# Loading the first batch's V by runs of four tokens, with half-height mask matmuls and grouped column sums

## The chip, the core and the metric

The kernel runs on one core of a Trainium2 chip. The metric is the device time of one execution in microseconds (us). TensorE is called PE in the profile (PEld is its weight load), VectorE DVE, ScalarE ACT, GpSimd POOL. SyncE, SP, issues the loads and stores; SPq is its queue of them.

## The reference

Sliding-window attention over 8 batches of 8 heads, 576 tokens and 64 channels, then a two-layer network over the 4608 tokens.

```python
scores = scale * np.matmul(q, k.transpose(0, 1, 3, 2))
mask = np.abs(pos[:, None] - pos[None, :]) <= 32
scores = np.where(mask, scores, -1000000000.0)
attn = np.exp(scores - np.max(scores, axis=-1, keepdims=True))
attn = attn / (np.sum(attn, axis=-1, keepdims=True) + 1e-09)
attn_out = np.matmul(attn, v)
x = np.ascontiguousarray(attn_out.transpose(0, 2, 1, 3)).reshape(B * S, H * D)   # 4608 x 512
h = x @ w_in                      # 512 x 2048
r = np.maximum(h, 0.0)
g = s * (r * r) + b               # s and b are single numbers
out = g @ w_out                   # 2048 x 512
```

Since `b` is one number, `b` times the sum of `w_out` over its 2048 rows is a constant row of the output. The kernel computes it apart (`constant`) and adds it at the end.

## The kernel before

**A planner writes the order.** The kernel calls `add(engine, function, cost, reads, writes, key, ...)` for each piece of work. `_Graph.plan` then simulates the five engines and the DMA queue with these costs and picks, for each engine, whichever ready piece starts first (by `key` where several could). `emit` writes each engine's instructions in this order, with semaphore waits only where a buffer's reader or writer on another engine asks for one. The order is fixed at build time. On the chip each engine works it off in sequence and stands still where the next piece isn't ready.

**Names.** In the code the batches are numbered from 0; the texts here say batch one for `b = 0` and batch two for `b = 1`. A unit is 128 tokens of a batch; each batch has four whole ones and a half. `s1` is the first layer: 512 of the 2048 hidden channels (a weight chunk `w0` to `w3`, each loaded in halves `a` and `b`) for a block of tokens, four matmuls to each 128 channels. `second` is the second layer, with seven products in place of eight (`TW` and `GSUM` hold the sums for it).

**The start.** q and k of batch one come by head pairs (`load_pair`, 256 KB each, four tokens to a partition, so in runs of 1 KB), are cast to bf16, transposed on PE (`turn_pair`) and multiplied (`pair_scores`). A mask goes into the score banks first: `SHUT`, which is 0 inside the window and -1e38 outside, is multiplied by the identity `IDENT`, and the score matmuls (64 x 64 tiles) add to it, so that the exponential on ACT gives zeros outside. `stir` adds matmuls of a matrix of ones, whose results are not used.

The other loads of batch one and the first half of `w_in` follow by a written list:

```python
ORDER0 = ("v0", "w0a", "v1", "t", "w0b", "v2", "v3", "w1a", "v4", "w1b")
```

"v0" to "v4" are the units of V (`load_v`: 128 tokens to the partitions, 8 heads to a partition, so runs of 256 B; then one cast each, `cast_v`, by the engine in `EV0`). "t" is the tail of q and k, tokens 512 to 575, in two halves of 64 partitions; `late_scores` needs it, and units 3 and 4 need that. After the list, `first_units` does the five units: the product with V into a PSUM bank, the division (`finish`), a transpose on PE, and the copy to `XT`, from which `s1` reads. `ORDER1` goes on with q, k and V of batch two, the other two chunks of `w_in`, and `w_out`. SP issues all of it from one queue, and a load waits until the casts have left its staging slot (`STG`, a ring).

**The column sums.** `constant` multiplies each 128 x 512 tile of `w_out` by the matrix of ones (16 matmuls of 512 columns into one bank), and DVE multiplies the result by `b`.

**PSUM.** Four pairs of banks: `W` (transposes at the start, then the first layer), `O`, `SC` and `AVN`.

The functions around the change, with the line numbers of the profile:

Of the kernel before, what the change touches and what calls it, by code (L numbers as in the profile page):

```python
# [5 lines left out]
F32 = mybir.dt.float32  # L6
I32 = mybir.dt.int32
BF16 = mybir.dt.bfloat16
# [19 lines left out]
ORDER0 = ("v0", "w0a", "v1", "t", "w0b", "v2", "v3", "w1a", "v4", "w1b")  # L28
# [20 lines left out]
EV0 = ("dve", "act", "pool", "dve", "pool")  # L49
# [6 lines left out]
        ("turn", 3, "q"): 1, ("turn", 3, "k"): 1, ("scores", 2): 1, ("scores", 3): 1, ("av", 0): 1}  # L56
# [266 lines left out]
def bass_sliding_window_symmetric__then__act_starrelu_kernel(  # L323
# [23 lines left out]
    with ExitStack() as es:  # L347
# [49 lines left out]
        IDENT = sb((128, 128), BF16, "ident")  # L397
        GT = [sb((128, 16, 512), BF16, "gt") for _ in range(2)]
# [4 lines left out]
        CVEC = sb((128, DM), F32, "cvec")  # L403
        SB128 = sb((128, 2), F32, "sb128")
# [93 lines left out]
        for p0 in (0, 64):  # L498
            band(MASK[p0:p0 + 64, :], ONESW[p0:p0 + 64, :], ("MASK", 0, p0), 0, 64, -96)

# [34 lines left out]
        def take(what, n):  # L535
            ring[what] += 1
            return (ring[what] - 1) % n
# [63 lines left out]

        def load_pair(name, pr, load_key):
# [7 lines left out]
        def stir(spot, res, view, key):  # L610

            n = STIR.get(spot, 0)
            if n:
                add("pe", [lambda e: e.matmul(view, lhsT=ONESW[:, :], rhs=ONESW[:, :].rearrange("p (one c) -> p one c", one=1)
                                              .to_broadcast((128, 4, 128)), start=True, stop=True) for _ in range(n)],
                    n * (427.0 if spot == ("turn", 0, "q") else 240.0), reads=["ONESW"], writes=[res], key=key - 0.05)
# [288 lines left out]
        def pair_scores(b, pr):  # L905
# [3 lines left out]
            if b == 0:  # L909
# [10 lines left out]
            add("pe", [lambda e, hp=hp: e.matmul(bank[:, hp, :], lhsT=IDENT[:, :], rhs=SHUT.rearrange("p u c -> p (u c)"),  # L920
                                                 start=True, stop=False, skip_group_check=True) for hp in (0, 1)],
                440.0, reads=["IDENT"] + [("SHUT", i) for i in range(4)], writes=[(name, 0), (name, 1)], key=key - 0.01)
# [72 lines left out]
        def attention():  # L995
# [228 lines left out]
        def constant():  # L1224

            for i in range(8):
                f0 = 2 * i
                add("pe", [lambda e, fc=fc: e.matmul(SC[:, 0, :], lhsT=ONESW[:, :], rhs=WOUT_BF[:, fc, :],  # L1228
                                                     start=(fc == 0), stop=(fc == 15)) for fc in (f0, f0 + 1)],
                    440, reads=["ONESW", ("Wout", i // 2, i % 2)], writes=[("SC", 0)], accum=i > 0, key=P2[0, 0] - 4.0 + 0.1 * i)  # L1230
            add("dve", lambda e: e.tensor_scalar(CVEC[:, :], SC[:, 0, :], SB128[:, 1:2], None, ALU.mult),
                680, reads=[("SC", 0), ("SB128", 1)], writes=[("CVEC", x) for x in (0, 1)], key=P2[0, 0] - 2.0)

# [273 lines left out]
```

## Time and profile before

| | |
|---|---|
| time, median of 3 runs | 308.14 us (307.1 to 309.0) |
| the profiled execution's own time | 308.89 us |
| its span in the profile | 307.2 us |
| PE busy | 294.9 us, 96% of the span |
| PEld busy | 213.4 us, 69% |
| DVE busy | 233.2 us, 76% |
| ACT busy | 156.7 us, 51% |
| POOL busy | 66.4 us, 22% |
| moved by the DMA engines | 54.30 MB, mean 177 GB/s |

How such a profile is read: the page gives busy times and groups of instructions. The chain of waits goes back from the last instruction, at each step to whatever released it. A row of a timeline has start, duration, engine, line of code, operation, output and inputs, count, and in brackets the idle time before it with what ended that; for PE, durations overlap, so the distance between starts says what a matmul costs. A row of a window has its length and then the busy time and number of instructions of PE, PEld, DVE, ACT and POOL, the TensorE clock granted (1.00 is full), the mean busy share of the 16 DMA engines, and GB/s.

### The profile page before, as it was taken

What the parts mean: (1) busy time and instruction counts of PE and PEld (TensorE: products, weight loads), DVE (VectorE), ACT (ScalarE), POOL (GpSimd) and SP (SyncE); (2) the same over time, 40 slices, a digit from 0 to 9 for tenths busy, and PEclk for the clock granted to TensorE, in tenths of its full rate; (3) what the DMA queues carried; (4) which work ended last, traced back from release to release, by engine and by line L of the source; (5) the groups of instructions that cost most, each with busy time, mean ns of one, the idle gap of its engine ahead of it and who ended that gap; (6) DMA issues with size and microseconds to landing.
All of it is one profiled execution on the core that took longest, in us unless ns stands there. A gap on an engine that the chain in (4) does not pass through costs nothing.

```text
span 307.2 us, 8786 instructions
## 1 busy us (share of the span) xinstructions
PE 294.9 (96%) x3837; PEld 213.4 (69%) x3837; DVE 233.2 (76%) x401; ACT 156.7 (51%) x244; POOL 66.4 (22%) x79
## 2 busy tenths in 40 slices
PE   8879899999999999999999999989999999999994
PEld 3458687798888887666766666656666666666783
DVE  3556788699879697989798768995877776566673
ACT  3746775685895564655554544542554433333200
POOL 5344587300000270055047000450000000000000
PEclk9979999999999999999999999999999999999999
DMA  7999999999994997999699679999513110210223
GB/s 204 290 246 302 325 291 370 268 227 273 159 232 125 239 202 160 279 201 178 184 255 198 132 172 273 186 201 150 153 21 88 53 47 31 74 34 2 69 70 107
DMA packets 120152, 54.30 MB, mean 177 GB/s; under 512 B 94816, under 2 KB 115936, under 8 KB 120112
## 3 DMA queue, kind: packets, MB, share of 16 engines
q1 hardware_dynamic: 120112, 53.72, 75.0%
q8 instruction: 31, 0.51, 0.8%
q14 instruction: 9, 0.07, 0.1%
HBM read 36.70 MB, written 9.44 MB: 150 GB/s over the span
## 4 chain that ended last, share of the span: by engine, by line
PE 79%; SPq 4%; DMA 3%; DVE 2%; issue 1%; POOL 0%
PE w L1097 36%; PE o L1154 31%; PE avn L839 4%; SPq L714 3%; DMA stg<-in_moe_w_in_dram 2%; PE sc L1154 2%; PE sc L781 2%; PE avn L870 1%; PE sc L1228 1%; DMA vst<-in_v_dram 1%; DVE outs L1170 1%; DVE gt L1110 1%; SPq L887 0%; SPq L707 0%; POOL win L564 0%
## 5 line engine op out<-in xcount | busy, mean ns | idle before, releaser
L1097 PE MATMUL w<-xt,win 128*128 128x512 bf16 (+4 forms) x832 | 145.7, 316 | 1.3 <-POOL win L564 1.3
L1104 ACT ACTIVATE r<-w 128x512 bf16<-128x512 f32 (+2 forms) x148 | 86.6, 586 | 105.6 <-PE w L1097 103.9
L1097 PEld LDWEIGHTS w<-xt,win 128*128 128x128 bf16 x832 | 75.6, 99 | 35.9 <-POOL win L564 1.9
L1110 DVE TENSOR_TENSOR gt<-r 128x1024 bf16<-128x1024 bf16 (+3 forms) x100 | 63.6, 639 | 24.9 <-ACT r L1104 24.2
L1154 PE MATMUL o<-wout,gt 128*128 128x256 bf16 x528 | 66.5, 273 | 0.0
L1154 PEld LDWEIGHTS o<-wout,gt 128*128 128x128 bf16 x528 | 50.8, 98 | 13.3
L733 POOL CAST nat<-stg 128x1024 bf16<-128x1024 f32 (+2 forms) x28 | 33.7, 1202 | 78.8 <-DMA stg<-in_q_dram 65.0
L809 ACT ACTIVATE ex<-sc 128x1024 bf16<-128x1024 f32 (+1 forms) x29 | 29.7, 1023 | 12.4 <-PE avn L839 10.8
L1154 PE MATMUL o<-tw,gt 128*128 128x256 bf16 x272 | 34.6, 273 | 0.0
L1154 PEld LDWEIGHTS o<-tw,gt 128*128 128x128 bf16 x272 | 26.2, 98 | 7.0
L1170 DVE SCALAR_TENSOR_TENSOR outs<-o,sb,cvec 128x512 f32<-128x512 f32 (+1 forms) x36 | 25.7, 715 | 4.3 <-PE o L1154 4.3
L1170 DVE SCALAR_TENSOR_TENSOR outs<-o,sb,outs 128x512 f32<-128x512 f32 (+1 forms) x27 | 19.3, 716 | 6.7 <-PE o L1154 6.6
L1146 DVE TENSOR_TENSOR gt<-gt 128x1024 bf16<-128x1024 bf16 (+1 forms) x26 | 23.8, 916 | 0.4
L813 DVE TENSOR_TENSOR ex<-ex,mask 128x1024 bf16<-128x1024 bf16 (+1 forms) x29 | 22.5, 775 | 0.6
L863 DVE TENSOR_TENSOR xn<-avn,rec 128x512 bf16<-128x512 f32 (+1 forms) x31 | 21.3, 687 | 0.7
L839 PE MATMUL avn<-vb,ex 64*64 64x65 bf16 x944 | 19.9, 197 | 1.9 <-issue 1.6
L839 PEld LDWEIGHTS avn<-vb,ex 64*64 64x64 bf16 x944 | 13.0, 106 | 11.5 <-issue 8.0
L598 DVE CAST vb<-vst 128x512 bf16<-128x512 f32 (+1 forms) x30 | 13.1, 444 | 9.5 <-DMA vst<-in_v_dram 9.5
L1154 PE MATMUL o<-tw,gsum 128*128 128x256 bf16 x136 | 17.7, 273 | 0.0
L1154 PEld LDWEIGHTS o<-tw,gsum 128*128 128x128 bf16 x136 | 12.8, 98 | 3.3
L1146 DVE TENSOR_TENSOR gsum<-gt 128x1024 bf16<-128x1024 bf16 x18 | 13.2, 731 | 0.3
L878 ACT COPY xt<-avn 128x512 bf16<-128x512 bf16 (+2 forms) x19 | 10.0, 533 | 4.8 <-PE avn L870 4.8
(119 smaller groups left out, 225.4 us busy)
## 6 DMA issues: line engine op xcount, KB each, us to landing
vst<-in_v_dram SPq DMA_DIRECT2D x32, 256.0 KB, 4.8
out_dram<-outs SPq DMA_DIRECT2D x32, 256.0 KB, 3.6
stg<-in_k_dram SPq DMA_DIRECT2D x24, 256.0 KB, 6.5
stg<-in_q_dram SPq DMA_DIRECT2D x5, 1024.0 KB, 6.0
stg<-in_moe_w_in_dram SPq DMA_DIRECT2D x8, 512.0 KB, 7.4
stg<-in_moe_w_out_dram SPq DMA_DIRECT2D x8, 512.0 KB, 7.4
stg<-in_q_dram SPq DMA_DIRECT2D x4, 512.0 KB, 8.2
stg<-in_k_dram SPq DMA_DIRECT2D x4, 512.0 KB, 8.4
```

Source lines behind the costliest of these rows:

```text
L598: (lambda e: e.tensor_copy(VB[0:n, vb, :, 0:D], VST[0:n, vs, :, :])),
L733: (lambda e, dst=dst, src=src: e.tensor_copy(dst, src)),
L809: add("act", lambda e, dst=flat_dst, src=flat_src: e.activation(dst, src, AF.Exp, bias=0.0, scale=0.125), 190 + 0.833 * 512 * len(hs), rea ...
L813: add("dve", lambda e, flat=flat, mask=mask: e.tensor_tensor(flat, flat, mask, ALU.mult), 130 + 0.53 * 512 * len(hs), reads=[("E", ei, hp, ...
L839: return [lambda e: e.matmul(av[64 * x:64 * x + 64, h, 0:D + 1], lhsT=buf[64 * g:64 * g + 64, h % 2, h // 2, c:c + 64], rhs=VB[64 * g:64 * ...
L863: add("dve", lambda e: e.tensor_tensor(XN[xi][0:p1, :].rearrange("p (a c) -> p a c", a=H), av[0:p1, :, 0:D], REC[ri][0:p1, :].rearrange("p ...
L1097: add("pe", [lambda e, g=g, kc=kc: e.matmul(wt[:, g, :], lhsT=WIN_BF[:, kc, (f0 + g) * 128:(f0 + g + 1) * 128], rhs=XT[:, kc, t0 % XR:t0 % ...
L1104: add("act", lambda e: e.activation(rt, wt, AF.Relu, bias=0.0, scale=1.0), 190 + 0.833 * ng * nt, reads=[("W", wb)], writes=[("R1", rb, ha ...
L1110: add("dve", lambda e: e.tensor_tensor(GT[gs][:, f1:f1 + nf, g0:g0 + nt], rr, rr, ALU.mult), 130 + 0.55 * nf * nt, reads=[("R1", rb, x) fo ...
L1146: add("dve", lambda e: e.tensor_tensor(dst, x, y, op), 1240.0 if half is None else 690.0, reads=reads, writes=writes, key=k)
L1154: add("pe", [lambda e, g=g, j=j, dst=dst: e.matmul(dst, lhsT=lhs[:, g, 128 * j:128 * j + 128], rhs=rhs[:, g, :], start=first and g == 0 an ...
L1170: add("dve", lambda e, src=src, dst=dst, other=other: e.scalar_tensor_tensor(dst, src, SB128[:, 0:1], other, ALU.mult, ALU.add), 200 + 1.0 ...
```

## The change

It has three parts.

**V of batch one.** The units 0 to 3 come in two loads ("va", "vb", 256 tokens each) instead of four. In each, four tokens in a row go to one partition, for four heads in partitions 0 to 63 and for the other four in 64 to 127, as two DMAs in runs of 1 KB. A cast on DVE brings all 128 x 1024 values to bf16. Sixteen matmuls of 32 rows with a constant pattern of zeros and ones (`SPREAD`) put each token on its own partition, in four banks; two evictions to a load bring them to `VB`. Unit 4 is loaded as before. The list of loads changes, and so does the filling ahead of unit 0 (`STIR`, one matmul to six), which now also waits for the first spread.

**The masks.** `SHUT` has the same rows for partitions 0 to 63 and 64 to 127. The two mask matmuls of a pair of banks now take 64 rows each, the first from the upper half, the second from the lower half, with `TWICE`, two 64 x 64 identities side by side.

**The column sums.** Four matmuls of 32 output columns go to four groups of 32 partitions of one bank, four rounds in all. ACT copies the four partial sums out, a float32 matmul with a matrix of 1/32 adds them up, and DVE multiplies by `b`.

```diff
-ORDER0 = ("v0", "w0a", "v1", "t", "w0b", "v2", "v3", "w1a", "v4", "w1b")
+ORDER0 = ("va", "vb", "w0a", "w0b", "t", "v4", "w1a", "w1b")
...
-EV0 = ("dve", "act", "pool", "dve", "pool")
+VCAST = ("dve", "dve")
+EV0 = ("act", "dve", "act", "dve", "pool")
...
-        ... ("av", 0): 1}
+        ... ("av", 0): 6}
...
+        for p0 in (0, 64):
+            add("dve", lambda e, p0=p0: e.tensor_copy(
+                TWICE[p0:p0 + 64, :].rearrange("p (a c) -> p a c", a=2),
+                IDENT[p0:p0 + 64, p0:p0 + 64].rearrange("p (a c) -> p a c", a=1).to_broadcast((64, 2, 64))), 120,
+                reads=["IDENT"], writes=[("TWICE", p0)], key=-95.5)
+        add("dve", lambda e: e.memset(SPREAD[:, :], 0.0), 200, ..., key=-59)
+        for u in range(4):
+            add("dve", lambda e, u=u: e.tensor_copy(
+                SPREAD[32 * u:32 * u + 32, :].rearrange("p (i x) -> p i x", i=4)[:, :, 0:128:4],
+                IDENT[32 * u:32 * u + 32, 32 * u:32 * u + 32]... .to_broadcast((32, 4, 32))), 150, ..., key=-59)
...
+        def load_runs(y, key):
+            for x in (0, 1):
+                add("sp", lambda e, x=x: e.dma_start(
+                    VST[64 * x:64 * x + 64, 2 * y:2 * y + 2, :, :]...,
+                    v[0, 4 * x:4 * x + 4, 256 * y:256 * y + 256, :].rearrange("h (p i) d -> p h (i d)", i=4)),
+                    600.0, writes=[("VSTH", y, x)] + ..., key=key + 0.1 * x, dma=("l", 16, 60.0))
+        def spread_runs(y, key, homes):
+            ni = take("nat", NNAT)
+            rows, eng = NAT[ni], VCAST[y]
+            ...    # the cast: 690 on DVE, slack 300
+            add("pe", [lambda e, i=i, u=u, x=x: e.matmul(
+                tile[u][:, x, 0:256], lhsT=SPREAD[64 * x + 32 * u:64 * x + 32 * u + 32, 128 * i:128 * i + 128],
+                rhs=rows[64 * x + 32 * u:64 * x + 32 * u + 32, 256 * i:256 * i + 256], start=(i == 0), stop=(i == 3))
+                for i in range(4) for u in (0, 1) for x in (0, 1)], 480.0, ..., key=key)
+            land["spread", y] = g.tasks[-1]
+            ...    # two evictions by EV0: 617 on ACT, 680 on DVE
...
-            add("pe", [lambda e, hp=hp: e.matmul(bank[:, hp, :], lhsT=IDENT[:, :], rhs=SHUT.rearrange("p u c -> p (u c)"),
+            add("pe", [lambda e, hp=hp: e.matmul(bank[:, hp, :], lhsT=TWICE[64 * hp:64 * hp + 64, :],
+                                                 rhs=SHUT[64 * hp:64 * hp + 64, :, :].rearrange("p u c -> p (u c)"),
                                                  start=True, stop=False, skip_group_check=True) for hp in (0, 1)],
-                440.0, reads=["IDENT"] + ...
+                240.0, reads=[("TWICE", 0), ("TWICE", 64)] + ...
...
-                stir(("av", u), res[0], bank[:, 0, :], -25.0 + u)
+                stir(("av", u), res[0], bank[:, 0, :], -25.0 + u, [land["spread", 0]])
...
+                elif t in ("va", "vb"):
+                    y = "ab".index(t[1])
+                    load_runs(y, nxt())
+                    spread_runs(y, -28.0 + 3 * y, (("AVN", AVN), ("W", W)))
...
         def constant():
-            for i in range(8):
-                f0 = 2 * i
-                add("pe", [lambda e, fc=fc: e.matmul(SC[:, 0, :], lhsT=ONESW[:, :], rhs=WOUT_BF[:, fc, :],
-                                                     start=(fc == 0), stop=(fc == 15)) for fc in (f0, f0 + 1)],
-                    440, ..., key=P2[0, 0] - 4.0 + 0.1 * i)
-            add("dve", lambda e: e.tensor_scalar(CVEC[:, :], SC[:, 0, :], SB128[:, 1:2], None, ALU.mult), 680, ...)
+            key = P2[0, 0] - 4.0
+            add("dve", lambda e: e.memset(PART[:, :], 1.0 / 32), 150, writes=["PART"], key=-20)
+            for r in range(4):
+                add("pe", [lambda e, r=r, c=c: e.matmul(SC[32 * c:32 * c + 32, 0, :], lhsT=ONESW[:, 0:32], rhs=WOUT_BF[:, 4 * r + c, :],
+                                                        start=(r == 0), stop=(r == 3), skip_group_check=True) for c in range(4)],
+                    300.0, reads=["ONESW"] + [("Wout", r, x) for x in (0, 1)], ..., key=key + 0.1 * r)
+            add("act", lambda e: e.copy(CVEC[:, :], SC[:, 0, :]), 617.0, ..., key=key + 0.5)
+            add("pe", lambda e: e.matmul(SC[:, 1, :], lhsT=PART[:, :], rhs=CVEC[:, :], start=True, stop=True), 1000.0, ..., key=key + 0.6)
+            add("dve", lambda e: e.tensor_scalar(CVEC[:, :], SC[:, 1, :], SB128[:, 1:2], None, ALU.mult), 680, ...)
```

More of the change, by code (lines that the diff above doesn't have):

```diff
@@ L397, in bass_sliding_window_symmetric__then__act_starrelu_kernel @@
         IDENT = sb((128, 128), BF16, "ident")
+        TWICE = sb((128, 128), BF16, "twice")
+        SPREAD = sb((128, 4 * 129), BF16, "spread")
         GT = [sb((128, 16, 512), BF16, "gt") for _ in range(2)]
@@ L403, in bass_sliding_window_symmetric__then__act_starrelu_kernel @@
         CVEC = sb((128, DM), F32, "cvec")
+        PART = sb((128, 128), F32, "part")
         SB128 = sb((128, 2), F32, "sb128")
@@ L608, in load_pair, with stir @@
                 600.0, writes=stgr, key=load_key, dma=("l", 16, 60.0))
-        def stir(spot, res, view, key):
+        def stir(spot, res, view, key, waits=()):
             n = STIR.get(spot, 0)
@@ L615, in stir @@
                                               .to_broadcast((128, 4, 128)), start=True, stop=True) for _ in range(n)],
-                    n * (427.0 if spot == ("turn", 0, "q") else 240.0), reads=["ONESW"], writes=[res], key=key - 0.05)
+                    n * (427.0 if spot == ("turn", 0, "q") else 240.0), reads=["ONESW"], writes=[res], key=key - 0.05, waits=waits)
         def turn_pair(name, pr, key, banks, eng, slack):
```

33 lines of the change are left out of this document (28 added, 5 removed).

## The prediction

> **What bounds the kernel now.** I read the page first, then PE's waits, then the chain of waits in order of time, then five-microsecond windows, and last the timelines of the start.
>
> ```profile
> span 307.2 us, 8786 instructions
> ...
> PE 294.9 (96%) x3837; PEld 213.4 (69%) x3837; DVE 233.2 (76%) x401; ACT 156.7 (51%) x244; POOL 66.4 (22%) x79
> ...
> PE 79%; SPq 4%; DMA 3%; DVE 2%; issue 1%; POOL 0%
> ...
> PE w L1097 <- POOL win L564: 1.3, 2, 1.0
> ...
> 29.26 6.22 DMA stg<-in_moe_w_in_dram
> 35.54 1.05 POOL win L564
> 36.63 0.94 PE w L1097 x8
> ...
> 25.00:30.00 5.00, 4.79 (x66) 4.38 (x65) 2.71 (x7) 3.39 (x8) 2.79 (x3) 1.00 1.11 329
> 30.00:35.00 5.00, 4.65 (x98) 4.20 (x96) 3.67 (x8) 4.38 (x8) 1.94 (x2) 1.00 1.10 348
> ...
> 50.00:60.00 10.00, 10.00 (x85) 7.49 (x84) 7.50 (x9) 5.28 (x10) 5.60 (x5) 1.00 1.14 300
> ...
> 80.00:120.00 40.00, 40.00 (x640) 34.02 (x638) 33.59 (x62) 26.29 (x40) 8.37 (x9) 1.00 0.95 180
> ```
>
> PE is busy for 96% of the span and makes 79% of the chain. The chain begins with a load: the second half of the third weight chunk lands at 35.5 us, POOL casts it, and at 36.63 the first layer goes on, after PE's longest wait for a weight (1.0). From there PE has work at every moment (40.00 of 40 us). Before it the DMA engines are full (share 1.10 to 1.11, the last column but one). So there are two regimes. Up to 36.63 time is worth what it takes off the **line of loads**; from 36.63 on, what it takes off **PE's own work**. The instructions of the early units of batch one count only where they reach past that wait.
>
> **The loads.** The order of loads is written out, and the engines work it off one after another, so each landing follows from the rows of the cast that waited for it.
>
> ```profile
> 9.52 1.02 DVE L623 CAST nat<-stg 128x512 bf16<-128x512 f32 x2
> ...
> 12.67 1.04 POOL L564 CAST win<-stg 128x1024 bf16<-128x1024 f32 x1 [2.75 <-DMA stg<-in_moe_w_in_dram]
> ...
> 15.26 0.61 POOL L646 CAST nat<-stg 128x512 bf16<-128x512 f32 x1 [1.55 <-DMA stg<-in_k_dram]
> ...
> 16.87 1.04 POOL L564 CAST win<-stg 128x1024 bf16<-128x1024 f32 x1 [0.99 <-DMA stg<-in_moe_w_in_dram]
> ...
> 19.45 0.43 DVE L598 CAST vb<-vst 128x512 bf16<-128x512 f32 x1 [2.33 <-DMA vst<-in_v_dram]
> ...
> 28.20 1.04 POOL L646 CAST nat<-stg 128x1024 bf16<-128x1024 f32 x1 [0.61 <-DMA stg<-in_q_dram]
> ...
> 31.19 1.04 POOL L646 CAST nat<-stg 128x1024 bf16<-128x1024 f32 x1 [1.96 <-DMA stg<-in_q_dram]
> ...
> 34.11 1.04 POOL L564 CAST win<-stg 128x1024 bf16<-128x1024 f32 x1 [1.87 <-DMA stg<-in_moe_w_in_dram]
> 35.54 1.04 POOL L564 CAST win<-stg 128x1024 bf16<-128x1024 f32 x1 [0.39 <-DMA stg<-in_moe_w_in_dram]
> ```
>
> Two weight halves in a row land 35.54 - 34.11 = 1.43 us apart. Between 16.87 and 19.45 lie only v2 and v3: 1.29 us each, for 256 KB in runs of 256 B. Between 12.67 and 16.87 lie v1, the tail load "t" and a weight half: (4.20 - 1.43) / 2 = 1.38 each for the two. Between 28.20 and 31.19 lie one k and one q load, 512 KB each in runs of 1 KB: 1.50 each. The change replaces four V loads in 256 B runs by two of 512 KB in 1 KB runs: 4 x 1.29 = 5.2 becomes 2 x 1.50 = 3.0. I take **2.2 us off every later landing**. SP issues four instructions for these two loads, as it did for the four, so its queue gets no longer; "t" and v4 now stand behind the first weight chunk in it. Bounds: nothing, if the halves (64 partitions each) go slower than whole loads, though "t", also in halves, is no slower than v2; and at most about 3.9, from the stretch below: its 219 GB/s beside 329 later is worth 5 x (1 - 219/329) = 1.7 more, if the mix of short runs is what slows it.
>
> ```profile
> 20.00:25.00 5.00, 4.86 (x95) 3.72 (x96) 4.39 (x9) 1.56 (x3) 1.73 (x2) 0.72 0.94 219
> ```
>
> So the chunk that lands at 35.5 comes at 33.3 and PE goes on at **34.4**. For this PE must be done with what stands ahead of it in its order.
>
> ```profile
> 20.30 2.90 PE L1097 MATMUL w<-xt,win 128*128 128x224 bf16 x16
> ...
> 23.36 0.72 PE L839 MATMUL o<-vb,ex 64*64 64x65 bf16 x32
> ...
> 20.00:20.50 0.50, 0.50 (x18) 0.40 (x19) 0.08 (x1) 0.00 (x0) 0.00 (x0) 0.50 0.86 205
> ```
>
> The first layer starts at 20.30 now, behind unit 2 of batch one, which waits for v2. In the new order the last k lands by 10.1 (two casts in a row from 9.52), then va 11.6, vb 13.1, the first weight chunk 14.5 and 16.0, its cast ends at 17.0. V no longer stands in the way, so the first layer starts near 17.3. From 20.30 to the stall that ends at 36.63 (1.05 long) PE has 15.3 us of work, part of it at half clock (0.50, the third column from the end); from 17.3 that ends at 32.6, ahead of 34.4 by 1.8. "t" lands near 17.3 instead of 15.26; unit 3, which needs it, now runs 8.1 us after that landing (23.36), and so by 25.4 at the latest, still ahead of 34.4 by 9 us. That is the cover for what the change adds at the front.
>
> **What the change adds at the front: nothing on the path.**
>
> ```profile
> 9.66 0.39 PE L614 MATMUL w<-onesw 128*128 128x512 bf16 x1 [0.35 <-DVE kt L633]
> 9.98 0.41 PE L914 MATMUL o<-qt,kt 64*64 64x128 bf16 x16
> 10.32 0.40 PE L628 MATMUL w<-ident,nat 128*128 128x128 bf16 x4
> ...
> L1104 ACT ACTIVATE r<-w 128x512 bf16<-128x512 f32 x11 | 6.6, 597 | 6.6 <-PE w L1097 6.4
> ...
> L646 DVE CAST nat<-stg 128x1024 bf16<-128x1024 f32 x2 | 1.4, 683 | 0.0
> ...
> L598 DVE CAST vb<-vst 128x512 bf16<-128x512 f32 x2 | 0.8, 422 | 2.3 <-DMA vst<-in_v_dram 2.3
> ...
> L863 DVE TENSOR_TENSOR xn<-o,rec 128x512 bf16<-128x512 f32 x4 | 2.7, 685 | 0.1
> ...
> 53.51 0.43 PE sc L1228 x2
> 53.94 0.87 PE w L1097 x8
> ```
>
> DVE: two casts of 683 ns, two evictions from PSUM near 685 in place of two casts of 422, and six short constant copies in its early idle time: 1.9 us. ACT: two evictions near 600 instead of one cast. PE: two spreads of 16 matmuls with 256 columns; eight such matmuls take 0.87 (L1097 x8), so 0.44 a spread when four run at once, 1.75 when none do. Five more filling matmuls of 512 columns cost 5 x 0.215 = 1.1 (two column sums of that size take 0.43). POOL loses v2's cast. All this is 2.0 us of PE and 1.9 us of DVE before 17.3, where the first layer waits for its weights anyway. I count 0; if that cover is gone it costs the 2.0 us of PE, of which the 1.8 us of slack ahead of 34.4 take all but 0.2.
>
> **Masks.** Two matmuls of 512 columns (0.43) become two on 64 rows each. The 16 score matmuls of 64 x 64 run from 9.98 to 10.32, that is 21 ns each where 128 columns alone take 54 (0.87 / 8 / 2): small tiles do run side by side. But the row before lasts 0.32 to the next start where the stream alone is 0.215: about 0.1 is lost on going over to small tiles. A mask goes from 0.43 to 0.215 + 0.1, saving 0.1. Eight are changed; only the last two of batch two lie at or behind the wait: **0.2 us**. Bounds: 0.45 saved (no loss on the change of tile) and 0.2 lost (no overlap).
>
> **Column sums.** Sixteen matmuls of 0.215 = 3.45 us go, in PE's full stretch (50 to 60 above). Four rounds come: 0.215 each if the four 32-column groups run at once, plus 0.1 to go over and perhaps some of it back; 0.37 a round, 1.5 together. Bounds 0.9 and 4.3 (one after another, with the switches). Then one float32 multiply of 512 columns, for which there is no row: at least 0.215 as for bf16, at most eight times that, 1.7. I take 1.0, the cost that the change writes down for its planner and the middle of the two. Its wait for ACT's copy lies under the first-layer matmuls that alternate with the sums. So 3.45 - 1.5 - 1.0 = **1.0 us saved**, bounds 2.3 saved and 2.5 lost.
>
> [...]
>
> **Sum.** 2.2 + 0.2 + 1.0 = 3.4 us. The profiled execution took 308.89 (span 307.2 and 1.7 around it), so 305.5; it lies 0.75 above the median of the runs shown, 308.14, so I predict **304.7**. Its own range, with the terms moving by half of their bounds, is 303.2 to 306.3.
>
> **Rivals.**
>
> *More is gained.* The loads gain 3.9 rather than 2.2, or the third and fourth score groups of batch two, which now run behind the wait though their transposes are done ahead of it, are placed ahead of it (0.35 each and a mask). For it: 219 GB/s at 20 to 25. Against: the landings measure 1.29 in that very stretch. 308.1 - 3.4 - 2.0 = 302.7.
>
> *The halves are no faster*, so that the change does not do what it says: only the PE terms stay, 308.1 - 1.2 = 306.9. For it: no load of half the partitions in 1 KB runs is in the trace. Against: "t".
>
> *The clock drops just before the weights come.*
>
> ```profile
> 18.00:18.50 0.50, 0.00 (x0) 0.00 (x0) 0.00 (x0) 0.50 (x2) 0.00 (x0) 1.00 0.45 126
> ...
> 22.50:23.00 0.50, 0.50 (x6) 0.45 (x4) 0.49 (x2) 0.06 (x1) 0.19 (x1) 0.70 0.82 190
> ```
>
> After an idle time near 18 the granted clock is 0.50 until about 22.7, some 3.5 us in which half the work, 1.7 us, is lost. Now PE gets more idle time between 17.3 and 34.4. If such a drop lies across 34.4, it costs up to 1.7: 306.4. For it: the six filling matmuls stand only ahead of unit 0. Against: score, transpose and weight work is spread over the stretch.
>
> [...]
>
> *Slower: the loads of a late batch slip.* The staging slots, NAT buffers and the written order all shift with the change.
>
> ```profile
> 186.00 1.03 SPq L714
> ...
> 187.08 3.12 SPq L714
> ...
> 190.24 3.20 SPq L714
> ...
> 193.48 0.81 SPq L714
> ...
> 208.09 0.32 PE L839 MATMUL avn<-vb,ex 64*64 64x65 bf16 x16 [1.62 <-issue]
> ```
>
> Four k loads hold SP's queue from 186.0 to 194.3, 8.3 us, and PE, which needs their scores, stands 1.62 us at 208. If these loads come one group later in SP's order, PE's wait grows by as much: 308.1 - 3.4 + 8.3 = 313.0. It is slower than before once the slip exceeds 3.4 us. For it: this is PE's one long wait behind 40 us. Against: the loads are released by PE's own progress, and move ahead with it.
>
> **How the numbers follow.** Forecast 0.51, more gained 0.14, halves no faster 0.10, clock 0.12, slower 0.13. A measurement of this kernel tells about 1% from no change, that is 305.06 and 311.2. Faster by over 1%: 0.14 and 0.32 of the forecast's 0.51, since its middle lies just under the line: 0.46. Slower by over 1%: 0.11 (the slip must exceed 6.5). The rest, 0.43, is within 1%. The range runs from 302.4 (the case of more gained, nearly whole) to 308.8 (halves and clock with 1.9 us of scatter), and leaves out most of the slower case and a little below: 0.17.
>
> **What would show it.** Right: the first layer starts near 17.3, the third chunk's last cast near 33.3 and PE behind it near 34.4, with column sums of some 2.5 us in all. Wrong in the loads: that cast within 1 us of 35.5. Wrong in the groups: a round of four takes near 0.87. Wrong in the clock: 0.50 at 30 to 38. Wrong as a whole: a wait of PE of over 4 us behind 60 us.

## The result and the profile after

| | before | after |
|---|---|---|
| median of 18 runs each | 308.24 us (307.03 to 310.89) | 310.39 us (308.36 to 311.90) |
| the profiled execution | 308.89 us, span 307.2 | 310.41 us, span 308.7 |

The ratio is **1.0059 (95% interval 1.0033 to 1.0084)**: the change makes the kernel slower by 1.8 us (the medians lie 2.15 apart). A run more than 1.5% above the fastest of its kernel is left out of every median and ratio here. The forecast was 304.7, in a range of 302.4 to 308.8.

The page of after seems to show PE busy for less time than before (293.2 us; 294.9). That is a trap: 27 of its matmul records are missing, as the count of weight loads beside it tells (3849 against 3876; both 3837 before). Busy times of PE can't be compared here, single rows can.

```profile
span 308.7 us, 8869 instructions
...
PE 293.2 (95%) x3849; PEld 212.9 (69%) x3876; DVE 237.6 (77%) x411; ACT 157.1 (51%) x246; POOL 63.5 (21%) x78
```

PE's waits of after (in total, times, longest). The head of the list is new:

```profile
PE w L708 <- POOL nat L694: 2.9, 1, 2.9
```

PE now stands 2.9 us for the transposes of the tail "t". In PE's timeline (start, duration, engine, line, output and inputs, count, idle time before) this wait, the first layer, a pair of masks, a common point (below) and the end of the second layer are:

```profile
22.66 0.61 PE L708 MATMUL w<-ident,nat 128*128 128x128 bf16 x4 [2.90 <-POOL nat L694]
...
25.36 1.68 PE L1150 MATMUL w<-xt,win 128*128 128x224 bf16 x8
...
28.18 0.39 PE L968 MATMUL sc<-shut,twice 64*128 64x512 bf16 x2
28.50 0.69 PE L887 MATMUL o<-vb,ex 64*64 64x65 bf16 x28
...
41.00 1.83 PE L1150 MATMUL w<-xt,win 128*128 128x224 bf16 x24
...
303.99 1.04 PE L1207 MATMUL sc<-tw,gt 128*128 128x256 bf16 x8
```

The common point and the end of the second layer before:

```profile
38.74 1.83 PE L1097 MATMUL w<-xt,win 128*128 128x224 bf16 x24
...
302.01 1.04 PE L1154 MATMUL sc<-tw,gt 128*128 128x256 bf16 x8
```

The rows at 38.74 and 41.00 can be compared: counted in the traces, the same first-layer columns, scores, masks, transposes and products with V lie ahead of both. (The first products of the second layer, at 61.56 and 63.36, can't: eight first-layer matmuls fewer lie ahead of that of after.) So after is 2.26 us behind at the common point and 1.98 behind at the last product: **in these two executions the loss lies ahead of 41 us**. Behind it after gains only 0.3, although the column sums there became shorter and PE's wait near 208 shrank from 1.62 to 0.26. The first layer starts at 25.36 instead of 20.30.

Windows of after (length, busy time and instructions of PE, PEld, DVE, ACT and POOL, clock granted, DMA share, GB/s) and the casts that the loads end in:

```profile
9.50:16.00 6.50, 5.59 (x94) 2.88 (x93) 3.01 (x6) 5.54 (x8) 0.61 (x1) 1.00 1.13 201
20.50:27.00 6.50, 4.15 (x66) 3.03 (x67) 1.54 (x3) 2.63 (x5) 4.07 (x5) 0.50 1.16 244
```

```profile
13.87 0.69 DVE L632 CAST nat<-vst 128x1024 bf16<-128x1024 f32 x1 [0.38 <-DMA vst<-in_v_dram]
16.82 0.69 DVE L632 CAST nat<-vst 128x1024 bf16<-128x1024 f32 x1 [2.26 <-DMA vst<-in_v_dram]
```

```profile
18.00 1.04 POOL L580 CAST win<-stg 128x1024 bf16<-128x1024 f32 x1 [6.94 <-DMA stg<-in_moe_w_in_dram]
20.35 1.04 POOL L580 CAST win<-stg 128x1024 bf16<-128x1024 f32 x1 [1.30 <-DMA stg<-in_moe_w_in_dram]
21.99 0.61 POOL L694 CAST nat<-stg 128x512 bf16<-128x512 f32 x1 [0.61 <-DMA stg<-in_k_dram]
...
36.95 1.07 POOL L580 CAST win<-stg 128x1024 bf16<-128x1024 f32 x1 [0.40 <-DMA stg<-in_moe_w_in_dram]
```

While V comes in (9.5 to 16), the DMA engines are full (1.13) and move **201 GB/s**, though the runs are 1 KB. V's second load lands at 16.82 (13.1 was forecast), "t" at 21.99 (17.3), the third chunk's second half at 36.95 (33.3; 35.54 before). The clock stands at 0.50 for these 6.5 us and a little longer; in the windows of before it was some 3.4.

### The profile page after: what moved, and what is told of

Its sections match the earlier page's. It is cut to its first block, busy times and chain, and to the rows that moved or that the text cites. A ratio compares the mean times of both kernels' runs of the same rounds, so it can differ in the third digit from the quotient of the medians.

```text
span 308.7 us, 8869 instructions
## 1 busy us (share of the span) xinstructions
PE 293.2 (95%) x3849; PEld 212.9 (69%) x3876; DVE 237.6 (77%) x411; ACT 157.1 (51%) x246; POOL 63.5 (21%) x78
## 4 chain that ended last, share of the span: by engine, by line
PE 71%; DMA 12%; SPq 6%; DVE 4%; POOL 3%; issue 2%; ACT 1%; POOLq 0%; ACTq 0%
PE w L1150 31%; PE o L1207 29%; DMA stg<-in_k_dram 6%; DMA stg<-in_moe_w_out_dram 5%; PE avn L887 3%; SPq L762 2%; PE sc L1207 2%; PE sc L829 2%; POOL nat L781 2%; DMA kt<-nat 1%; SPq L653 1%; PE avn L918 1%; SPq L621 1%; PE avn L721 1%; DVE outs L1223 1%
## 5 line engine op out<-in xcount | busy, mean ns | idle before, releaser
L1150 PE MATMUL w<-xt,win 128*128 128x512 bf16 (+4 forms) x805 | 139.2, 313 | 2.9 <-issue 1.7
L1150 PEld LDWEIGHTS w<-xt,win 128*128 128x128 bf16 x832 | 74.4, 98 | 32.9 <-ACT r L1157 0.6
L1163 DVE TENSOR_TENSOR gt<-r 128x1024 bf16<-128x1024 bf16 (+3 forms) x100 | 62.8, 636 | 24.8 <-ACT r L1157 24.1
L781 POOL CAST nat<-stg 128x1024 bf16<-128x1024 f32 (+2 forms) x28 | 32.2, 1151 | 79.7 <-DMA stg<-in_q_dram 66.2
L1199 DVE TENSOR_TENSOR gt<-gt 128x1024 bf16<-128x1024 bf16 (+1 forms) x26 | 24.5, 942 | 0.4
L861 DVE TENSOR_TENSOR ex<-ex,mask 128x1024 bf16<-128x1024 bf16 (+1 forms) x29 | 21.3, 736 | 1.4 <-ACT ex L857 0.3
L614 DVE CAST vb<-vst 128x512 bf16<-128x512 f32 (+1 forms) x28 | 12.1, 435 | 4.0 <-DMA vst<-in_v_dram 4.0
L1199 DVE TENSOR_TENSOR gsum<-gt 128x1024 bf16<-128x1024 bf16 x18 | 14.4, 798 | 0.3
```

The lines of the kernel that those rows point to most:

```text
L614: (lambda e: e.tensor_copy(VB[0:n, vb, :, 0:D], VST[0:n, vs, :, :])),
L781: (lambda e, dst=dst, src=src: e.tensor_copy(dst, src)),
L861: add("dve", lambda e, flat=flat, mask=mask: e.tensor_tensor(flat, flat, mask, ALU.mult), 130 + 0.53 * 512 * len(hs), reads=[("E", ei, hp, ...
L1150: add("pe", [lambda e, g=g, kc=kc: e.matmul(wt[:, g, :], lhsT=WIN_BF[:, kc, (f0 + g) * 128:(f0 + g + 1) * 128], rhs=XT[:, kc, t0 % XR:t0 % ...
L1163: add("dve", lambda e: e.tensor_tensor(GT[gs][:, f1:f1 + nf, g0:g0 + nt], rr, rr, ALU.mult), 130 + 0.55 * nf * nt, reads=[("R1", rb, x) fo ...
L1199: add("dve", lambda e: e.tensor_tensor(dst, x, y, op), 1240.0 if half is None else 690.0, reads=reads, writes=writes, key=k)
```

## The experiments

Ratios are to the kernel before, each with its 95% interval; 1% is 3.1 us. A "whole" version loads V in 128 partitions: "va" is heads 0 to 3 and "vb" heads 4 to 7, of all 512 tokens.

### Which part of the change costs

```diff
 e1_pe_only: before + masks + sums        e2_masks: before + masks
 e1_v_only:  after - masks - sums         e2_sums:  before + sums
```

> The kernel before with the masks on 64 rows and the grouped column sums only; V is loaded as before. All theories of the V load: the loads land as in the kernel before (third chunk's last cast near 35.5), the column sums with their float32 multiply take about 2.1 us of PE instead of 3.5, a mask pair 0.32 instead of 0.43: 306.3 to 307.3. If it is 308 or more, the planner's new order or the longer chain of the sums eats the gain, and the changed kernel's loss isn't V's alone.

> The changed kernel with the masks and the column sums of the kernel before: V's part alone. If the parts add up: 310.4 plus about 1.4, so 311.5 to 312. If it is near 310, the masks and sums brought nothing within the changed kernel; near 308, the loss comes from the two together.

> The kernel before with the grouped column sums alone. If PE's own work sets the end behind 36 us, as the prediction has it, the sums take 2.1 us instead of 3.5 and the time falls by 1.0 to 1.4 us, to 307.0 to 307.4 (ratio 0.996). If the saving is given back in waits behind it (ACT's copy and DVE's multiply now lie in that stretch, and the order is written anew), the time stays within 0.5 us of 308.4.

> The kernel before with the half-height mask matmuls alone. By the prediction only two of the eight pairs lie on the path: 0.2 us less, no difference that can be seen, 308.2 within 0.7. If the two constant copies on DVE at the start or the order written anew cost something, 309 to 310.

| | median us | ratio |
|---|---|---|
| masks and sums | 308.68 | 1.0024 (0.9995 to 1.0053) |
| V alone | 311.21 | 1.0096 (1.0066 to 1.0127) |
| sums alone | 307.66 | **0.9969 (0.9941 to 0.9997)** |
| masks alone | 308.70 | 1.0012 (0.9979 to 1.0045) |

V costs, the sums gain, the masks do nothing that can be seen. Beside V alone, the changed kernel (1.0059) is 0.4% faster, about what masks and sums were expected to bring in it, though the two intervals overlap. The version with the sums alone beats both kernels. Its timeline shows a round, what follows it, and the float32 multiply:

```profile
57.70 0.40 PE L1230 MATMUL sc<-wout,onesw 128*32 128x512 bf16 x4
58.03 1.92 PE L1098 MATMUL w<-xt,win 128*128 128x256 bf16 x16
59.79 1.02 PE L1234 MATMUL sc<-cvec,part 128*128 128x512 f32 x2
60.65 0.39 PE L661 MATMUL avn<-ident,nat 128*128 128x128 bf16 x4
```

A round lasts 0.33 to the next start, the multiply 0.86: 4 x 0.33 + 0.86 = 2.2 us in place of 3.45, a saving of 1.25; 0.31% of 308.3 is 0.96, with an interval of 0.1 to 1.8. The float32 multiply's 0.86 is four times the 0.215 of 512 columns in bf16 (before, two column sums from 53.51 to 53.94). Masks and sums together do not show this gain; why the two do not add up was not settled.

### Do halves load slower, and does it matter?

```diff
 e1_whole (after, V loads):
-    for x in (0, 1): VST[64*x:64*x+64, ...] <- v[0, 4*x:4*x+4, 256*y:256*y+256, :]
+    VST[:, 2*y:2*y+2, ...] <- v[0, 4*y:4*y+4, 0:512, :]
 e1_half_q (before, the q and k pairs at the start):
-    stg <- src[0, 2*pr:2*pr+2, 0:512, :]
+    for x in (0, 1): stg[64*x:64*x+64, :] <- src[0, 2*pr:2*pr+2, 256*x:256*x+256, :]
```

> The changed kernel, with its two V loads cut otherwise: each takes 512 tokens for four heads, so one DMA over all 128 partitions in runs of 1 KB, in place of two DMAs of 64 partitions each; 32 rows then belong to one unit, and each eviction moves 4 heads of two units. Bytes, run length, place in the order, number of casts, spread matmuls and evictions stay. Theory 'halves' (a load that fills 64 partitions at a time moves at some 205 GB/s): the second V load's cast starts near 13 instead of 16.82, the last cast of the third weight chunk near 33.5 instead of 36.95, time 304 to 306. Rival 'runs' (1 KB runs of V, or 512 KB loads at this place, are slow however they are cut): landings as in the changed kernel, 310. Rival 'order' (the loss is the tail load standing behind both weight halves): V lands earlier, yet PE still waits some 3 us for the tail's cast and the time stays within 1 us of 310.

> The kernel before, with each of the eight first q and k loads (256 KB in runs of 1 KB, 128 partitions) issued as two DMAs of 64 partitions, same bytes to the same places. Theory 'halves': a load takes about 1.25 instead of 0.75 us, the last k lands near 14 instead of 10.1, and the rate at 3 to 12 us falls from about 340 to about 210 GB/s. Rivals 'runs' and 'order': only SP's issue time grows (8 more instructions of 0.45), and the rate stays near 340 where q and k alone move.

Windows (columns as above; the last is GB/s) of the kernel with half loads of q and k, with two rows of SP's timeline, then of before, then of the whole version:

```profile
3.00:12.00 9.00, 8.19 (x74) 3.82 (x71) 3.26 (x9) 4.15 (x6) 2.85 (x10) 1.00 0.70 199
...
3.55 1.26 SPq L605 DMA_DIRECT2D stg<-in_q_dram  x2
4.86 1.25 SPq L605 DMA_DIRECT2D stg<-in_k_dram  x2
```

```profile
3.00:12.00 9.00, 8.63 (x82) 4.35 (x80) 4.72 (x12) 4.84 (x7) 3.68 (x11) 1.00 1.05 307
```

```profile
9.00:15.00 6.00, 5.56 (x91) 2.77 (x91) 3.83 (x7) 5.15 (x8) 1.29 (x2) 1.00 1.10 366
18.50:25.00 6.50, 5.13 (x74) 4.22 (x75) 2.99 (x5) 3.38 (x7) 3.73 (x5) 0.51 1.13 300
```

After and the whole version move the same bytes in the same runs at the same place of the list, with full DMA engines in both (1.13 and 1.10): 201 GB/s in halves, 366 in whole loads. So **the halves are slower** here; what makes them so, no run shows.

The half loads of q and k (one run, 312.7 us) add no proof, though their rate fell from 307 to 199: SP issues two halves, 256 KB, every 1.31 us, which is 200 GB/s by itself, and the DMA engines are busy for 0.70 only.

But the speed did not matter for the time. Theory 'halves' had the landings right and its 304 to 306 us wrong. In the whole version the third chunk's second half is cast at 33.08, 3.9 us earlier than after. Its POOL timeline, its PE waits, and its PE timeline at the first layer, at the common point and further on:

```profile
33.08 1.04 POOL L580 CAST win<-stg 128x1024 bf16<-128x1024 f32 x1 [0.27 <-DMA stg<-in_moe_w_in_dram]
```

```profile
PE w L707 <- POOL nat L693: 1.9, 1, 1.9
```

```profile
22.49 3.13 PE L1149 MATMUL w<-xt,win 128*128 128x224 bf16 x16
...
38.78 0.41 PE L828 MATMUL sc<-qt,kt 64*64 64x128 bf16 x8
...
49.62 0.40 PE L917 MATMUL o<-ident,xn 128*128 128x128 bf16 x4 [1.32 <-DVE xn L910]
```

PE waits for no `w_in` chunk any more; the time is 310.03 us, ratio 1.0057 (1.0026 to 1.0087), the same as after. PE stands 1.9 us for "t", the clock is halved from 18.5 to 25 (0.51), and the first layer starts at 22.49, at half clock (16 matmuls in 3.13).

Yet at 38.78 PE has done the work of the common point, so it is level with before (38.74) and 2.2 us ahead of after. The whole version loses its time behind that: its last product comes at 302.94 (302.01 before) in spite of the shorter sums. A row of its DVE timeline and a window of it, then the same window of before:

```profile
40.32 0.91 DVE L860 TENSOR_TENSOR ex<-ex,mask 64x1024 bf16<-64x1024 bf16 x1 [2.44 <-ACT ex L856]
...
40.00:50.00 10.00, 8.36 (x212) 6.82 (x206) 9.65 (x18) 5.29 (x12) 7.96 (x9) 1.00 1.01 318
```

```profile
40.00:50.00 10.00, 9.61 (x242) 8.12 (x240) 8.35 (x22) 6.74 (x14) 7.72 (x11) 1.00 1.09 321
```

DVE, in its written order, stands 2.44 us for an exponential, then has no pause (9.65 of 10 us), and PE stands 1.32 us for its division. No run isolates this part of the loss; that the order, written anew for each version, makes it is likely but not shown.

### What are the loads worth at all?

```diff
 e5_nov (before, batch one): v2 and v3 are not loaded; their casts read v0's and v1's staging
 e4_noload (before, batch two): the second halves of q and k are not loaded; their casts read the first halves' staging
```

> The kernel before without the loads of V units 2 and 3 of batch one; their casts read units 0 and 1 instead, so that all other work stays (the products of units 2 and 3 use the wrong V). That is 2 x 1.29 = 2.6 us less in the line of loads, no more work on any engine, and no wait for v2 at 18. Theory L (the loads bound the start): every later landing 2.6 us earlier, PE goes on behind the third chunk near 34.0, and the time falls by 2 to 2.6 us, to 306 to 306.5. Theory P (PE's own chain bounds it; the loads are worth only the wait of 1.05): the third chunk's last cast near 33, no wait for it, and the time falls by 0 to 1.1 us, to 307.5 or more.

> The kernel before without two loads of batch two, the second halves of q and k (512 KB each, in runs of 1 KB, 1.5 us each in the line of loads ahead of the third weight chunk); their casts read the first halves' staging, so that all other work stays (batch two's heads 4 to 7 use the scores of heads 0 to 3). Theory L, the prediction's (up to 36.6 us time is worth what it takes off the line of loads): the third chunk's last cast comes at 32.5 instead of 35.5, PE goes on behind it 3 us earlier, and the time falls by 3 us to 305.3. Theory P (PE's own chain bounds the start; the loads are worth only PE's wait of 1.05 for that chunk): the cast comes at 32.5 too, the wait is gone, and the time falls by at most 1.1 us, to 307.2 or more.

POOL's casts, PE's rows and a window of the kernel without v2 and v3:

```profile
33.73 1.04 POOL L564 CAST win<-stg 128x1024 bf16<-128x1024 f32 x1 [1.14 <-DMA stg<-in_moe_w_in_dram]
```

```profile
20.08 3.17 PE L1100 MATMUL w<-xt,win 128*128 128x224 bf16 x16
...
37.37 1.83 PE L1100 MATMUL w<-xt,win 128*128 128x224 bf16 x24
...
52.78 0.61 PE L1231 MATMUL sc<-wout,onesw 128*128 128x512 bf16 x2 [0.63 <-POOL wout L564]
...
56.31 0.60 PE L1231 MATMUL sc<-wout,onesw 128*128 128x512 bf16 x2 [0.46 <-POOL wout L564]
...
50.00:60.00 10.00, 8.80 (x68) 6.12 (x67) 6.33 (x10) 4.79 (x10) 3.61 (x4) 1.00 1.12 283
```

Without v2 and v3 the third chunk's cast starts at 33.73 (35.54 before). PE has no wait at its use. Its row at 37.37 is the common point again (38.74 before): PE is 1.37 us ahead there, a little more than the wait of 1.05. Time 308.33 us, **ratio 0.9985 (0.9959 to 1.0011)**: 2.6 us of loads less are worth 0.5 us, at most 1.3. That excludes theory L's 2 to 2.6 us, the point on which the prediction fell, and has the size of theory P. It does not show theory P's reason, PE's own chain: in the profiled execution (309.71 us) PE lost the lead again, in part by standing for the casts of `w_out`, the next loads, in a stretch where before it was busy for 10.00 of 10 us. The last product came at 303.13 (302.01 before). The other kernel, 310.78 us, 1.0062 (1.0032 to 1.0093), settles nothing, since its loads did not come earlier: those of its third chunk waited in SP's queue for staging slots until 31.6, and the second half's cast came at 35.50 again.

### "t", the fillings, the clock, the order

```diff
 e2_whole_t:    whole, ORDER0 = va vb t w0a w0b v4 w1a w1b
 e3_whole_t0:   whole, ORDER0 = t va vb w0a w0b v4 w1a w1b
 e5_whole_o2:   whole, ORDER0 = va w0a vb t w0b w1a v4 w1b
 e2_bef_t:      before, ORDER0 = v0 w0a v1 w0b v2 v3 t w1a v4 w1b
 e3_whole_fill: whole, 8 filling matmuls ahead of t's transposes
 e3_t0_fill:    e3_whole_t0, STIR ("av", 1): 4, ("av", 2): 8
 e4_whole_s1:   whole, STIR ("av", 0): 1
 e3_sums_fill:  e2_sums, STIR ("av", 2): 8
 e4_cost:       before, the cost of a mask pair that the planner reads: 240 for 440
```

> The whole-load version with one more change: in the written list the tail t stands ahead of both halves of the first weight chunk (va vb t w0a w0b v4 w1a w1b). Theory A (the gain of the faster V loads is lost because PE, in its written order, waits for t behind two weight halves, and the idle time of 1.9 us at 18 to 20 brings the half clock over the whole of the work that follows): t's cast starts near 16 instead of 19.12, PE's wait for it goes from 1.9 to under 0.5, the half clock lasts under 3 us instead of 6, the first layer starts by 20.5 instead of 22.49, and the time falls by 1.5 to 3 us below the whole-load version, to 307 to 308.5. Theory B (the order of the later part, written anew with every change, decides): the front improves as in A but the time stays within 1 us of 310.0. Theory C (the extra work of the spread, six fillings and evictions, is what costs): the first layer still starts behind 22 and the time stays near 310.

> The kernel before with one thing changed: the tail t goes behind the first weight chunk and v2, v3 in the written list (v0 w0a v1 w0b v2 v3 t w1a v4 w1b); V loads, masks and sums as before. Theory A (a late t costs by itself): t's cast moves from 15.26 to 18 to 19, PE stands 1 to 3 us for it, the half clock lasts longer than 3.5 us, and the time rises by 1 to 2.5 us, to 309.4 to 311. Theory B (t has slack of several us, as the prediction counted: unit 3 runs 8 us behind its landing): no wait for t over 0.5 us and a time within 0.7 us of 308.4.

> The whole-load version with eight filling matmuls (512 columns, 1.7 us at full clock) put right ahead of the transposes of the tail t, where PE stood 1.9 us. Theory A (the half clock that follows the idle time eats the gain of the loads): no 0.50 between 18 and 26, the first layer's first 16 matmuls take 1.6 us instead of 3.1, some 3 us of PE work are won back, and the time falls from 310.0 to 307 to 308.5 with the first product of the second layer 1 to 3 us earlier than without the filling. Theory B (the later part's order decides): the clock is full, but the time stays within 0.8 us of 310.0.

> The whole-load version with the tail t as the first of the list (t va vb w0a w0b v4 w1a w1b): t's transposes and the late scores then stand in PE's order ahead of the first spread, and nothing waits for t later. Theory A (wait for t and half clock): the first layer starts at 19 to 20.5, as soon as the second half of the first weight chunk is cast; if the clock still drops while PE waits for that weight, half of the gain is lost, and the time is 308 to 309.5; without the drop 306.5 to 308. Theory B (later order): within 0.8 us of 310.0. Theory C (V comes 1.4 us later and the exponentials' consumers with it): the first layer starts behind 22.

> The same as the version with t first, with fillings of four and eight matmuls ahead of units 1 and 2 of batch one, so that PE has no idle time of 2 us between 15 and 21. Theory A: no half clock, the first layer's 16 matmuls take 1.6 us, the third weight chunk (about 33) is what PE waits for, and the time is 305.5 to 307.5, below both kernels. Theory B: within 0.8 us of 310.0. Theory C (the fillings themselves delay the units by their 2.6 us): first layer behind 22 and no gain over the version with t first alone.

> The kernel before with the grouped column sums and with eight filling matmuls ahead of unit 2 of batch one, into PE's idle time at 18 to 19.4; V and masks as before. The half clock at 19.4 to 22.7 should be gone. If the loads bound the start, as the prediction read it from PE's wait for the third weight chunk, the 1.7 us won only make that wait longer (1.0 becomes 2 to 3 us) and the time stays where the sums alone have it, 307.7 within 0.6. If PE's own work bounds the start, it falls by 1 to 1.7 us, to 306.0 to 306.7.

> The whole-load version with the list in the old order: va w0a vb t w0b w1a v4 w1b. If t's place costs it the gain (it waits 1.9 us for t now, with the half clock behind), t's cast comes near 17.5 and w0b near 19; the first layer starts by 21 and the time is 307.5 to 309. If the spread and DVE's casts and evictions of V cost it, the first layer starts at 22 or later and the time stays at 309.5 to 310.5.

> The whole-load version with one filling ahead of unit 0 instead of six, as in the kernel before. If the five fillings (1.1 us of PE) are on PE's path, the time falls from 310.0 to about 308.9. If they lie under the wait for ACT's eviction of the first spread (PE stands 0.69 at 16.0 there) and for t, it stays within 0.5 us of 310.0; if the clock halves earlier for want of them, it rises by 1 us or more.

> The kernel before with the same instructions; only the cost of a pair of mask matmuls that the planner reads is 240 instead of 440 ns, so that it writes another order (some of the first transposes, scores and fillings, and later the loads of batches 4 and on relative to each other). Theory B (the written order of the rest moves the time by 1 to 2 us, whatever the change): 307 or less, or 309.4 or more. Theory P (the order of the rest matters little, the first 35 us decide): within 0.7 us of 308.3.

| | median us | ratio |
|---|---|---|
| e2_whole_t | 310.10 | 1.0051 (1.0020 to 1.0081) |
| e3_whole_t0 | 312.39 | 1.0133 (1.0087 to 1.0178) |
| e5_whole_o2 | 310.14 | 1.0037 (1.0005 to 1.0069) |
| e2_bef_t | 313.33 | 1.0165 (1.0127 to 1.0203) |
| e3_whole_fill | 309.86 | 1.0080 (1.0048 to 1.0111) |
| e3_t0_fill | 313.72 | 1.0177 (1.0136 to 1.0219) |
| e4_whole_s1 | 310.64 | 1.0053 (1.0030 to 1.0076) |
| e3_sums_fill | 310.09 | 1.0064 (1.0035 to 1.0094) |
| e4_cost | 309.19 | 1.0014 (0.9979 to 1.0050) |

My theory A (the wait for "t" and the half clock behind it eat the gain) fell. The filled wait did what it should, and something else followed. PE's timeline and two windows of it:

```profile
17.67 1.90 PE L661 MATMUL w<-onesw 128*128 128x512 bf16 x8
...
21.01 0.94 PE L1152 MATMUL w<-xt,win 128*128 128x224 bf16 x8
...
28.48 0.61 PE L920 MATMUL o<-ident,xn 128*128 128x128 bf16 x4 [1.43 <-DVE xn L913]
```

```profile
18.50:25.00 6.50, 5.96 (x111) 4.36 (x109) 3.18 (x7) 4.48 (x10) 3.45 (x5) 1.00 1.13 311
28.00:31.50 3.50, 2.96 (x18) 2.03 (x18) 2.56 (x6) 1.46 (x3) 1.42 (x2) 0.57 1.11 350
```

The clock is full from 18.5 to 25 and the first layer starts at 21.01, at full speed; then PE stands 1.43 us for DVE's division, and the clock drops there (0.57 from 28 to 31.5). So the drop was moved, not avoided, and the fillings took 1.7 us themselves. The sums version with fillings did keep its clock, and became slower than the sums alone. Its window, then that of the sums alone:

```profile
14.00:42.00 28.00, 24.38 (x504) 18.68 (x500) 19.01 (x33) 19.46 (x36) 14.71 (x17) 1.00 1.12 299
```

```profile
17.50:23.50 6.00, 4.86 (x71) 3.64 (x69) 2.80 (x5) 3.55 (x7) 2.69 (x3) 0.50 0.99 248
```

The sums alone, the fastest kernel of all, thus have a half clock about as long as after's. V alone, no faster than after, had the highest mean clock of the three in its profiled execution: 0.995, against 0.987 in after and 0.993 before.

Fewer fillings (e4_whole_s1) and "t" ahead of the first weight chunk (e2_whole_t) changed nothing against the whole version's 1.0057. "t" as the first of the list cost 2 us more, and nearly 4 with fillings. In the old order (e5_whole_o2) the first layer started at 23.42 and the time stayed near 310, the second of its two readings, which points to V's longer way rather than to the place of "t". "t" later, in the kernel before, cost 5 us; PE then stood for the weight behind it, among others:

```profile
27.15 1.83 PE L1097 MATMUL w<-xt,win 128*128 128x224 bf16 x24 [1.68 <-POOL win L564]
```

So a late "t" is dear, though the prediction gave it 9 us of cover. Another order with the same instructions (e4_cost) moved the time by no more than its interval, 0.5%; it is one order of many.

### The longer way of V

```diff
 e6_way (before, batch one's units 0 to 3):
-    cast:  VB[vb] <- VST[u]
+    cast:  VTMP[u % 2] <- VST[u]
+    PE:    bank <- IDENT x VTMP[u % 2]          # 512 columns; AVN for 0, 1, W for 2, 3
+    evict: VB[vb] <- bank                       # ACT for 0, 2, DVE for 1, 3
```

> The kernel before, its loads, list, masks and sums unchanged; only V's units 0 to 3 of batch one take the longer way: after the cast they go through a matmul with the identity (512 columns) into the banks that the spread uses, and ACT (units 0, 2) or DVE (1, 3) evicts them to the place where the products read them. Added: 0.9 us of PE, about 1.2 us of ACT and 1.4 us of DVE. Theory W (the longer way of V delays the units, and with them the first layer, which PE's own chain cannot make up): the first layer starts 1 us or more behind 20.3 and the time rises by 1.5 to 3 us, to 310 to 311.5. Theory F (the front has cover, as the prediction counted): within 0.7 us of 308.5, and what slows the versions with the spread is the written order around it.

PE's timeline up to the first layer (clock 0.50 from 20.5 to 27, so durations are long) and the third chunk's cast:

```profile
19.92 1.13 PE L603 MATMUL w<-vtmp,ident 128*128 128x512 bf16 x2 [0.90 <-POOL vtmp L600]
20.98 0.95 PE L851 MATMUL sc<-vb,ex 64*64 64x65 bf16 x32
...
23.14 0.95 PE L851 MATMUL o<-vb,ex 64*64 64x65 bf16 x32 [0.67 <-DVE rec L873]
...
24.55 0.93 PE L851 MATMUL avn<-vb,ex 64*64 64x65 bf16 x24
25.42 1.68 PE L1109 MATMUL w<-xt,win 128*128 128x224 bf16 x8
```

```profile
35.30 1.04 POOL L565 CAST win<-stg 128x1024 bf16<-128x1024 f32 x1 [0.45 <-DMA stg<-in_moe_w_in_dram]
```

The loads are those of before and the third chunk lands as before (35.30). Yet the first layer starts at 25.42, as in after, behind units 2 and 3, and the time is 313.40 us, **ratio 1.0154 (1.0122 to 1.0187)**, 4.7 us more. Part of the later start is order: before starts the first layer behind unit 2, this kernel behind unit 4. But PE does not make it up: the time shows that the longer way of V, with the order that is written around it, is enough by itself to slow the kernel. That it costs more here than in after (four steps instead of two, a later place of units 2 and 3) was not taken apart further.

## Why the prediction was wrong, step by step

**The regime ("up to 36.63 time is worth what it takes off the line of loads").** This step failed first. The 1.05 us wait for the third chunk was read as a sign of a long stretch bounded by loads, with PE at work at every moment behind it. Taking 2.6 us of loads away gave 0.5 us, at most 1.3. With those loads gone PE passed the common point 1.4 us earlier, about the wait's own length, and did not keep the lead: it met waits for `w_out` that it had not had. The whole version had the third chunk 3.9 us and the common point 2.2 us ahead of after, and the same time; it stood for DVE. Why a lead is lost there, and in every version anew, stays open.

**The cover ("all this is 2.0 us of PE and 1.9 us of DVE before 17.3", priced at 0).** It rested on a first layer that starts at 17.3. V's new way lies between its load and units 0 to 3, and the first layer stands behind units 0 to 2 in PE's written order: it started at 25.36, or 22.49 with whole loads. After came to the common point 2.26 us late, where the prediction had it early. e6_way prices the way, with its order, at 4.7 us.

**The loads, 2.2 us.** The bound "nothing, if the halves go slower" was named and set aside because "t", in halves too, is no slower than v2. But both of these come in 256 B runs; no row had halves in long runs. They ran at 201 GB/s, where the whole loads ran at 366, and the third chunk came 1.4 us later instead of 2.2 earlier. The size was wrong; by the whole version a right size would not have brought the time either.

**The tail "t" (9 us of cover).** Its cast came at 21.99, and PE stood 2.9 us for it, since its transposes stand ahead of units 2 and 3 in the order; the cover was counted from the unit that uses the scores, not from the first instruction in PE's order that needs the load.

**The clock.** That it would fall was foreseen as a rival, at 306.4; it fell earlier than at 34.4, for over 6.5 us instead of 3.4. It does not carry the loss: the sums alone have about the same half clock as after and are faster than before, V alone had the higher mean clock and is no faster than after, and with the clock kept (e3_sums_fill) the time did not fall.

**Masks and sums held.** A pair lasts 0.32 (28.18 to 28.50), as forecast. The sums were put at 2.5 us and took 2.2. The float32 multiply in them was put at 1.0 and took 0.86; its upper bound, eight times bf16, was the author's estimate, and the one ratio that a run shows is four (0.86 to 0.215). Of the sums' gain, 1.0 us was forecast and 0.96 measured (0.1 to 1.8), in the kernel with the sums alone.

**The rivals and the range.** *The halves are no faster* had the loads right, and put 306.9 because it priced the rest of V's change at nothing. No rival was a loss by V's longer way. *More gained* and *slower by slipping loads* did not come: PE's wait near 208 shrank to this:

```profile
210.06 0.32 PE L887 MATMUL avn<-vb,ex 64*64 64x65 bf16 x16 [0.26 <-DMA kt<-nat]
```

The forecast's own range, up to 306.3 "with the terms moving by half of their bounds", is narrower than its bounds make it: half of them is 1.1 for the loads, 0.2 for the masks and 1.75 for the sums, 3.05 together, so 307.8, or 306.8 if the three are independent.

## What to carry to other kernels

A wait at the end of a long stretch says how much can be won at that point, not that the stretch is bound by what it waits for: try it by leaving the load out, and see how much of the lead is still there further on. Compare two kernels at rows that have the same work ahead of them; a first product or a first layer can stand behind more work in one order than in the other. A test with more and smaller loads has to be checked for the time that issuing them takes (here 1.31 us for two halves of q or k). Faster loads that put casts, matmuls and evictions between a load and its first reader can lose more than they bring, and with a fixed order the slack of a load runs to the first instruction that needs it, not to the result it ends in.

## What was not expected of the hardware

Loads into 64 partitions moved 201 GB/s where the same bytes into 128 moved 366, both with full DMA engines (1.13 and 1.10). A load of q or k into 64 partitions took SP about 0.6 us to issue (two in 1.26), one of twice the bytes into 128 took 0.47. A float32 multiply of 512 columns took 0.86 us, four times the 0.215 of bf16. The half clock lasted about 3.4 us in before (19.4 to 22.8) and about twice that (6.0 to 6.5 in the windows shown, and a little more) in after, the whole version, e6_way and the sums alone. What sets these lengths, no run shows; in before PE was busy for 2.00 of the 4 us from 16 to 20, the stretch in which the clock fell.
